# A second channel fold in the Fourier mixing of an attention and feed-forward kernel, with pooled rows packed into idle partitions and the local part added when the tokens are read back

## The chip, the cores and the metric

The kernel runs on one core of one Trainium2 chip. The metric is the device time of one execution in microseconds (us). A core has five engines with queues of their own, which run in order and wait for each other by semaphores: TensorE (PE; its weight loads are a row of their own, PEld), VectorE (DVE), ScalarE (ACT), GpSimd (POOL) and SyncE (SP), which here only issues DMAs. POOL issues some DMAs too, those that add to what lies at the destination.

## The reference

```python
# q, k, v: (8 batches, 8 heads, 576 positions, 64)
q_d, k_d, v_d = means of 4 neighbouring positions        # 144 groups
out_up    = repeat(softmax(q_d k_d^T / 8) v_d, 4)        # "pooled" attention
out_local = softmax(q k^T / 8 where |i - j| < 4) v       # "local" attention
x = (out_up + out_local) as (8, 576, 512)
u = x + real(fft(fft(x, axis=1), axis=2))                # sequence, then channels
un = (u - mean(u)) / sqrt(var(u) + 1e-6)                 # over the 512 channels
out = u + relu(un @ w1) @ w2                             # w1 512 x 2048, w2 2048 x 512
```

## The kernel before

For each batch the work has three parts: five units of local attention (`Unit`; a unit is two windows of 64 positions for all heads), four steps of pooled attention (`Pooled`; two heads each), and the mixing (`Mix`). The feed-forward (`Block`) follows, over nine blocks of 512 tokens and 16 slices `f` of the hidden layer. All fp32 products of the mixing and the feed-forward are made of three products of high and low parts (`fh` and `fl`, `yh` and `yl`, `hh` and `hl`).

No scheduler orders the instructions. Each class has a `plan` that puts its steps on a list with a number as its time (`at`), in units of a pace of 20 per batch; the list is sorted once, and each engine's queue is the sorted list cut down to that engine. The table `AT` holds the numbers. They set an order and nothing else.

The mixing, which the change is about, goes as follows. Local results lie in `xa` (positions of the first half) and `xb` (the second half, mirrored), as 3 slots of 128, 128 and 64 rows; the upper 64 rows of slot 2 hold zeros. `half_sum` (DVE) and `half_difference` (POOL) make `xs` and `xm`, the even and odd parts over the sequence. Pooled results lie in `odt`: 72 rows by 2, for the first and the mirrored second half. `channels_even` and `channels_odd` (DVE) fold the 512 channels into 256 sums and 256 differences (`xeo`); `split_high` (ACT) and `split_low` (POOL) make `fh` and `fl`. `sequence` then multiplies by cosines and sines over the sequence, in four groups `T` of 128 channels: 3 products of 5 slots (2 pooled slots of 72 rows, 3 local), 15 matmuls of 320 columns each, 60 in all; channel 256, which the fold leaves out, goes through `sequence_z` apart. `mix` multiplies by cosines and sines over the channels: for each of the 3 slots of output rows 7 matmuls of 512 columns for the even part and 6 for the odd, 39 in all. `mixed` (DVE) adds half of `xs` or `xm` to each, from PSUM (L611), `unfold` (POOL) makes sum and difference of the two (L621), and `store` (SP) writes these to `um` in DRAM, in 10 DMAs (L634, L635). The pooled results go to `ud` in DRAM, four copies of each row (L332, L336).

The feed-forward reads its tokens back: a load from `um` (SP, L706), and on top of it an adding load from `ud` (POOL, L704). The first block's tokens `ut` are loaded once the pooled part of the last batch is through (`close_b`, time `t_b`), and its norms begin at `t_a`, when the last local unit is through. The weights come as 64 `Quarter`s, each through a DMA (`raw`, L146), ACT, POOL, DVE (three instructions, L169 to L175), ACT and POOL; 12 of them are done during the attention, the others from `t_a` on.

A batch's queries and keys come by five DMAs (`qkT`, L361, on SP), and `sums` (DVE, L379) makes the pooled ones of them, for which the first product of a pooled step (`sp`, L262, on PE) waits.

Of the kernel before, what the change touches and what calls it, by code (L numbers as in the profile page):

```python
# [65 lines left out]
def kernel(  # L66
# [11 lines left out]
    c_group: bass.AP,  # L78
# [28 lines left out]
    um = [dram.tile([S + 1, DM], F32, name=f"um{b}") for b in range(B)]  # L107
# [21 lines left out]
    nc.vector.memset(mhalf, -0.5)  # L129
    ident = res.tile([P, P], F32, name="ident")  # L130
# [74 lines left out]
    odt = pd.tile([GH, 2, DM + 2], F32, name="odt")  # L205
# [34 lines left out]
    class Pooled:  # L240
# [74 lines left out]
        def result(self, h0):  # L315
# [7 lines left out]
                out=odt[:, :, h0 * D : (h0 + 2) * D].rearrange("g t (h d) -> g t h d", h=2),  # L323
# [4 lines left out]
        def store(self):  # L328

            for t in range(2):  # L330
                r0 = t * (HS + 1)
                nc.sync.dma_start(  # L332
                    out=ud[self.b][r0 : r0 + HS, :].rearrange("(g r) c -> g r c", r=4),
                    in_=odt[:, t, :DM].unsqueeze(1).to_broadcast([GH, 4, DM]),
                )
            nc.sync.dma_start(out=ud[self.b][HS : HS + 1, :], in_=odt[GH - 1 : GH, 1, :DM])  # L336

        def plan(self):
# [8 lines left out]
            at(pooled_end(b) + AT["store_pooled"][0], self.store)  # L347

# [143 lines left out]
    halves = [[pf.tile([P, NSL, DM + 2], F32, name=f"x{h}{i}") for h in "sm"] for i in range(2)]  # L492
    for t in (t for ts in halves for t in ts):
        nc.gpsimd.memset(t[:, :, DM:], 0.0)
    slots = [(t, P if t < NSL - 1 else W) for t in range(NSL)]

    def constants():
# [3 lines left out]
        nc.gpsimd.dma_start(out=seqg, in_=c_group)  # L501
# [4 lines left out]
    class Mix:  # L506


        def __init__(self, b):
            self.b, self.x, self.y = b, {}, {}  # L510
            self.fh = self.z = None


        def half_sum(self, t):
            self.xs, self.xm = halves[self.b % 2]
            nc.vector.tensor_add(out=self.xs[:, t, :DM], in0=xa[:, t], in1=xb[:, t])

# [5 lines left out]
        def source(self, t, odd):
            if t < NSL:
                return halves[self.b % 2][odd][:, t]
            return odt[:, t - NSL]

        def channels_even(self, t):
            x, src = psq.tile([P, DM], F32, name="xeo", bufs=2), self.source(t, 0)
            x = self.x[t] = x[: src.shape[0]]  # L530
            nc.vector.tensor_add(out=x[:, 0:HD], in0=src[:, 0:HD], in1=src[:, DM:HD:-1])
# [504 lines left out]
```

## Time and profile before

| | |
|---|---|
| median of 3 runs (lowest to highest) | 1250.11 us (1248.47 to 1251.0) |
| profiled execution: its time, its span | 1254.06 us, 1252.0 us |
| mean granted TensorE clock of that execution | 0.967 |
| busy PE, PEld | 1184.1 us (95%), 981.2 us (78%) |
| busy DVE, ACT, POOL | 590.7 us (47%), 356.0 us (28%), 318.2 us (25%) |
| DMA | 111.45 MB, mean 89 GB/s |

Every time below is from the profiled execution and counts from the start of its span. "Busy" is the time in which an engine had an instruction running; "idle before" is the gap ahead of an instruction and what ended it. A matmul's duration overlaps the next one's, so the price of a matmul in a row is the length of the row divided by their number. In the lines shown, names stand as written<-read; a row of a group ends with its busy time, the mean of one in ns, and the idle time before it with who ended it. The five last matmul groups of local values (`av`, L452) of a batch mark the end of its attention: they end at 56.7, 105.3, 157.7, 208.8, 258.8, 303.5, 348.7 and 389.0 us.

### The profile page before, as it was taken

Reading aid. Unit: us, or ns where it says so; the run is one execution under the profiler, and the core shown is the slowest. Engines: PE = TensorE matmul, PEld = TensorE weight load, DVE = VectorE, ACT = ScalarE, POOL = GpSimd, SP = SyncE. Lnnn points to the kernel's source line nnn. Section 1 sums busy time; section 2 is a strip of 40 time slices with the busy share of each in tenths; the row PEclk is TensorE's granted clock in tenths of the full one; section 3 lists DMA queues with packets and bytes.
Section 4 is the critical chain, followed back from the end, with each engine's and each line's share of the span. In section 5 each row is a group of like instructions: output and inputs, shape, how many; then the busy total and the mean of one; then the engine's idle time right before and its main releaser. Section 6 shows DMA issues by size and latency. Waiting matters only on the chain.

```text
span 1252.0 us, 20525 instructions
## 1 busy us (share of the span) xinstructions
PE 1184.1 (95%) x8336; PEld 981.2 (78%) x8336; DVE 590.7 (47%) x1218; ACT 356.0 (28%) x1038; POOL 318.2 (25%) x397
## 2 busy tenths in 40 slices
PE   5889998899995699999999999999999999999998
PEld 5777887787984578888888888888888888888887
DVE  3767778698877788853222222122122222221211
ACT  3655454555562333431111111111011111111100
POOL 2226355365456566531010010000100100100000
PEclk7888998999997799999999999999999999999999
DMA  9755484565645525314040120210400400300000
GB/s 293 197 169 134 128 238 110 162 196 172 163 127 153 133 77 155 119 51 101 5 97 1 52 50 1 78 25 1 99 3 1 101 1 1 101 1 1 34 1 34
DMA packets 50462, 111.45 MB, mean 89 GB/s; under 512 B 6120, under 2 KB 6248, under 8 KB 50040
## 3 DMA queue, kind: packets, MB, share of 16 engines
q1 hardware_dynamic: 42000, 88.66, 22.6%
q0 software_dynamic: 8368, 21.48, 9.3%
q8 instruction: 66, 1.08, 0.4%
q14 instruction: 28, 0.23, 0.1%
HBM read 81.82 MB, written 28.34 MB: 88 GB/s over the span
## 4 chain that ended last, share of the span: by engine, by line
PE 81%; DVE 10%; DMA 6%; POOL 1%; SPq 1%; issue 1%; ACT 1%; POOLq 0%
PE hps L761 31%; PE acc L779 10%; PE acc L781 10%; PE acc L780 10%; PE y L569 4%; PE mix L607 4%; DMA vsum<-in_vg_dram 3%; PE av L452 2%; DMA qkT<-in_qk_dram 2%; PE avd L307 2%; PE sc L393 1%; DVE sums L379 1%; DVE xeo L535 1%; PE tpn L732 1%; PE sp L262 1%
## 5 line engine op out<-in xcount | busy, mean ns | idle before, releaser
L761 PE MATMUL hps<-unT,w1h 128*128 128x512 f32 x1152 | 311.5, 392 | 0.6 <-DVE yl L578 0.6
L769 DVE SCALAR_TENSOR_TENSOR hl<-hps,hh 128x512 fp32r<-128x512 f32 x144 | 99.3, 690 | 437.3 <-ACT hh L765 437.3
L761 PEld LDWEIGHTS hps<-unT,w1h 128*128 128x128 f32 x1152 | 215.2, 188 | 46.7 <-DVE yl L578 0.8
L765 ACT ACTIVATE hh<-hps 128x512 fp32r<-128x512 f32 x144 | 86.2, 598 | 512.1 <-PE hps L761 512.0
L779 PE MATMUL acc<-w2h,hh 128*128 128x512 f32 x576 | 226.5, 393 | 0.0
L781 PE MATMUL acc<-w2h,hl 128*128 128x512 f32 x576 | 225.1, 391 | 0.0
L780 PE MATMUL acc<-w2l,hh 128*128 128x512 f32 x576 | 225.0, 391 | 0.0
L761 PE MATMUL hps<-unT,w1l 128*128 128x512 f32 x576 | 155.2, 391 | 0.0
L761 PEld LDWEIGHTS hps<-unT,w1l 128*128 128x128 f32 x576 | 108.1, 188 | 23.8
L781 PEld LDWEIGHTS acc<-w2h,hl 128*128 128x128 f32 x576 | 108.2, 188 | 23.6
L779 PEld LDWEIGHTS acc<-w2h,hh 128*128 128x128 f32 x576 | 108.1, 188 | 22.9
L780 PEld LDWEIGHTS acc<-w2l,hh 128*128 128x128 f32 x576 | 108.2, 188 | 22.8
L717 POOL TENSOR_TENSOR rstd<-rstd,mhalf 128x1 f32<-128x1 f32 x36 | 20.3, 564 | 341.4 <-DVE rstd L716 341.4
L704 POOL DMA_DIRECT2D ut<-ud x40 | 35.5, 1111 | 208.0 <-DMA ut<-um 207.7
L607 PE MATMUL mix<-chanm,yh 128*128 128x512 f32 (+1 forms) x192 | 65.8, 425 | 5.6 <-DVE xs L611 3.7
L411 ACT ACTIVATE sb<-sc,mx 128x64 f32<-128x64 f32 x320 | 69.8, 329 | 1.3
L741 DVE TENSOR_TENSOR unT<-tpn,unT 128x512 fp32r<-128x512 f32 x36 | 24.8, 690 | 90.4 <-ACT unT L738 90.4
L547 POOL TENSOR_TENSOR fl<-xeo,fh 128x512 fp32r<-128x512 f32 (+1 forms) x40 | 56.0, 1404 | 30.5 <-ACT fh L542 30.2
L379 DVE TENSOR_REDUCE sums<-qkT 128x224 f32<-128x896 f32 (+4 forms) x48 | 44.5, 947 | 27.9 <-DMA qkT<-in_qk_dram 19.6
L520 POOL TENSOR_TENSOR xm<-xa,xb 128x512 f32<-128x512 f32 x24 | 34.2, 1427 | 87.9 <-DVE xb L470 79.9
L738 ACT CAST unT<-tpn 128x512 fp32r<-128x512 f32 x36 | 21.0, 586 | 113.5 <-PE tpn L732 113.5
L452 PE MATMUL av<-vaug,pT 64*64 64x65 f32 x1280 | 48.5, 227 | 1.7 <-DVE odt L322 1.5
(102 smaller groups left out, 1579.7 us busy)
## 6 DMA issues: line engine op xcount, KB each, us to landing
qkT<-in_qk_dram SPq DMA_DIRECT2D x40, 512.0 KB
raw<-in_wq_dram SPq DMA_DIRECT2D x64, 256.0 KB
vaug<-in_vw_dram SPq DMA_DIRECT2D x40, 260.0 KB
ud<-odt SPq DMA_DIRECT2D x16, 576.0 KB
out_dram<-ut SPq DMA_DIRECT2D x36, 256.0 KB
ut<-um SPq DMA_DIRECT2D x32, 256.0 KB
ut<-ud POOLq DMA_DIRECT2D x32, 256.0 KB, 5.6
vsum<-in_vg_dram POOLq DMA_DIRECT2D x24, 292.5 KB, 4.5
```

The costliest lines, as they stand in the source:

```text
L379: nc.vector.tensor_reduce(out=to, in_=x[:, :, a - g0 : e - g0], axis=AX.X, op=ALU.add)
L411: nc.scalar.activation(out=self.sb[:, a], in_=self.sc[:, a * W : (a + 1) * W], func=AF.Exp, scale=0.125, bias=self.mx[:, a : a + 1],)
L452: nc.tensor.matmul(av[r, a, :], pT[r, 4 * hh + a], va[r, 4 * hh + a, :], start=True, stop=True)
L547: nc.gpsimd.tensor_sub(out=l, in0=self.x[t], in1=h.bitcast(F32))
L569: nc.tensor.matmul(y, l, r, start=(i == 0), stop=(i == len(mms) - 1))
L607: nc.tensor.matmul(to, l, r, start=(i == 0), stop=(i == len(mms) - 1))
L761: nc.tensor.matmul(hps, a[:, c, :], unT[:, x, c, :], start=(i == 0), stop=(i == len(mms) - 1))
L765: nc.scalar.activation(out=hh, in_=self.hps[f], func=AF.Relu)
L769: nc.vector.scalar_tensor_tensor(out=hl, in0=self.hps[f], scalar=0.0, in1=self.hh[f].bitcast(F32), op0=ALU.max, op1=ALU.subtract)
L779: nc.tensor.matmul(acc, hh, w2h, start=start, stop=False)
L780: nc.tensor.matmul(acc, hh, w2l, start=False, stop=False)
L781: nc.tensor.matmul(acc, hl, w2h, start=False, stop=stop)
```

## The change

The mixing is folded over the channels a second time. `channels` makes 255 sums and 255 differences into `w`; `fold` adds `w` to its own mirror image (DVE) and subtracts it from it (POOL), which leaves four groups of 128 channels, each of which reaches only the even or only the odd output channels. Two channels (0 and 256) now go through `sequence_z`. In `mix` each group has a product of 256 columns in place of 512: 1 matmul of 512 columns and 6 of 256 for the even part, 6 of 256 for the odd. `pack` moves the pooled results of the mirrored half by two SBUF to SBUF transfers: 56 rows into the idle rows 72 to 127 of `odt`, 16 rows into the idle rows 64 to 79 of `xa`'s slot 2. With that the pooled part is one slot, and a `sequence` group has 12 matmuls in place of 15.

`mixed` is gone. `even_out` (ACT) copies the even part from PSUM, and `unfold` (DVE) makes sum and difference of that copy and the odd part in PSUM, interleaving the two halves of 256 channels on the way. The local results are no longer added there: `store` writes `xa` and `xb` to a third DRAM tensor `ux` (10 more DMAs per batch on SP), and every block is loaded in three parts: `um` (SP), then adding loads from `ux` and from `ud` (POOL). `xs` and `xm` have one buffer each in place of two; the matrices of the channels shrink from 2 MB to 1 MB.

The first block's tokens have memory of their own from the start, and their loads are spread over the times 120 to 167; its norms begin at `t_b`, and the memory for its transposed tokens is there at `t_b` too.

```diff
-    "mix": (18.44, 18, 18),
+    "mix": (25.73, 25.9, 24.42, 25.37, 25.13),
-    "qk": (-11.61, 2.5),
+    "qk": (-10, 1.23),
...
+        def pack(self):
+            n = P - GH
+            nc.sync.dma_start(out=odt[GH:, 0, :DM], in_=odt[:n, 1, :DM])
+            nc.sync.dma_start(out=xa[W : W + GH - n, NSL - 1, :], in_=odt[n:GH, 1, :DM])
...
+        def channels(self, t, odd):
+            if self.w.get(t) is None:
+                self.w[t] = psq.tile([P, 2, HD], F32, name="w", bufs=2)
+            src = odt[:, 0] if t == NSL else halves[odd][:, t]
+            nc.vector.tensor_tensor(
+                out=self.w[t][:, odd, 1:HD], in0=src[:, 1:HD], in1=src[:, DM - 1 : HD : -1],
+                op=ALU.subtract if odd else ALU.add)
+        def fold(self, t, minus):
+            if self.x.get(t) is None:
+                self.x[t] = psq.tile([P, 4, P], F32, name="xeo", bufs=2)
+            eng, op = (nc.gpsimd, ALU.subtract) if minus else (nc.vector, ALU.add)
+            w = self.w[t]
+            eng.tensor_tensor(out=self.x[t][:, 2 * minus : 2 * minus + 2, :],
+                in0=w[:, :, 1 : P + 1], in1=w[:, :, HD - 1 : P - 1 : -1], op=op)
...
         def slots(self, x, odd, i):
-            groups = [(x[:GH, NSL + t], seqg[:, i, odd, t, :]) for t in range(2)]
-            return groups + [(x[:, t], seqm[:, i, odd, t, :]) for t in reversed(range(NSL))]
+            return [(x[:, t], seqm[:, i, odd, t, :]) for t in (NSL, NSL - 1, *range(NSL - 1))]
...
         def mix(self, t, odd):
-            for T in (2 * odd, 2 * odd + 1):
-                mms += [(lh, mh), (lh, ml), (ll, mh)]
-            if not odd:
-                mms.append((yz[:, cols], signs.unsqueeze(1).to_broadcast([P, HD, 2])))
+            if not odd:
+                sg = signs.unsqueeze(2).to_broadcast([P, 2, HD])
+                nc.tensor.matmul(to, yz[:, cols], sg, start=True, stop=False, skip_group_check=True)
+            for half, T in enumerate((3, 1) if odd else (0, 2)):
+                to = ps[:, half * HD : (half + 1) * HD]
+                for i, (l, r) in enumerate(((lh, mh), (lh, ml), (ll, mh))):
+                    nc.tensor.matmul(to, l, r, ...)
...
-        def mixed(self, t, odd):
-            x = (self.xm if odd else self.xs)[: slots[t][1], t, :DM]
-            nc.vector.scalar_tensor_tensor(out=x, in0=x, scalar=0.5, in1=self.ps, op0=ALU.mult, op1=ALU.add)
+        def even_out(self, t):
+            even = self.even[t] = pf.tile([P, DM], F32, name="even", bufs=2)
+            nc.scalar.copy(out=even[: slots[t][1]], in_=self.ps[t, 0])
-        def unfold(self, t):
-            for o, op in zip((oa, xm), (ALU.add, ALU.subtract)):
-                nc.gpsimd.tensor_tensor(out=o[:, t, :DM], in0=xs[:, t, :DM], in1=xm[:, t, :DM], op=op)
+        def unfold(self, t, minus):
+            even, ps = (x.rearrange("p (two n) -> p n two", two=2) for x in (self.even[t][:n], self.ps[t, 1]))
+            nc.vector.tensor_tensor(
+                out=self.o[minus][:n, t].rearrange("p (n two) -> p n two", two=2),
+                in0=even, in1=ps, op=ALU.subtract if minus else ALU.add)
...
+            at(..., self.store, ux, (xa, xb))
...
-                if pooled:
-                    nc.gpsimd.dma_start(out=u[r0 : r0 + m], in_=ud[b][k0 : k0 + m, :], accum_op=ALU.add)
+                src = (um, ux, ud)[part][b][k0 : k0 + m, :]
+                if part:
+                    nc.gpsimd.dma_start(out=u[r0 : r0 + m], in_=src, accum_op=ALU.add)
                 else:
-                    nc.sync.dma_start(out=u[r0 : r0 + m], in_=um[b][k0 : k0 + m, :])
+                    nc.sync.dma_start(out=u[r0 : r0 + m], in_=src)
...
-            at(t_b + 0.1 + 0.1 * i + AT["add"][0] * pooled, blocks[0].load, i, pooled)
+            at(120 + AT["add"][0] * part + 4 * i, blocks[0].load, i, part)
...
-            (blocks[0], t_a, AT["first_norms"]),
+            (blocks[0], t_b, AT["first_norms"]),
```

The table gives the queues another order at three places that matter below. The first is SP's queue in the middle of the program, around the five loads of the sixth batch's queries and keys. In the kernel before, where one of the loads has gone ahead of these rows and two follow:

```order
L361 DMA qkT<-in_qk_dram 128x1024
L634 DMA um_67<-oa 56x3x512
L634 DMA um_67<-oa 3x1x512
L634 DMA um_67<-oa 56x2x512
L634 DMA um_67<-oa 2x1x512
L635 DMA um_67<-oa 4x512
L634 DMA um_67<-xm_134 56x3x512
L634 DMA um_67<-xm_134 3x1x512
L634 DMA um_67<-xm_134 56x2x512
L634 DMA um_67<-xm_134 2x1x512
L635 DMA um_67<-xm_134 3x512
L361 DMA qkT<-in_qk_dram 128x1024
```

And in the changed kernel, the same place (line numbers are its own; `xb` is the local result, `o` the mixed one), where one load and the five stores of `xa` have gone ahead:

```order
L654 DMA ux_68<-xb 56x3x512
L654 DMA ux_68<-xb 3x1x512
L654 DMA ux_68<-xb 56x2x512
L654 DMA ux_68<-xb 2x1x512
L655 DMA ux_68<-xb 3x512
L375 DMA vaug<-in_vw_dram 128x520
L149 DMA raw<-in_wq_dram 128x512
L371 DMA qkT<-in_qk_dram 128x1024 x3
L375 DMA vaug<-in_vw_dram 128x520
L371 DMA qkT<-in_qk_dram 128x1024
L654 DMA um_75<-o_2982 56x3x512
```

Before, three of the five loads stand behind the store of the mixed rows; now four stand behind the store of the local results, and the mixed rows follow all five.

The second is VectorE's queue from the last pooled result of a batch to the folds. Before:

```order
L322 TENSOR_TENSOR odt<-avd,rsd 72x2x128
L406 TENSOR_REDUCE mx<-sc 128x8
L531 TENSOR_TENSOR xeo<-odt 72x256
L611 SCALAR_TENSOR_TENSOR xs_133<-xs_133,mix 128x512
L535 TENSOR_TENSOR xeo<-odt 72x256
L516 TENSOR_TENSOR xs_135<-xa,xb 128x512
L531 TENSOR_TENSOR xeo<-odt 72x256
L535 TENSOR_TENSOR xeo<-odt 72x256
```

And in the changed kernel, where `w` is what `channels` writes and `xeo` what `fold` writes:

```order
L325 TENSOR_TENSOR odt<-avd,rsd 72x2x128
L416 TENSOR_REDUCE mx<-sc 128x8
L476 TENSOR_SCALAR rs<-av 128x4 x2
L477 RECIPROCAL rs<-rs 128x8
L480 TENSOR_TENSOR xb<-av,rs 128x256 x2
L535 TENSOR_TENSOR w<-odt 128x255
L593 TENSOR_TENSOR yl<-y,yh 128x320
L535 TENSOR_TENSOR w<-odt 128x255
L548 TENSOR_TENSOR xeo<-w 128x256
L270 TENSOR_REDUCE mxd<-sp 72x2 x2
L636 TENSOR_TENSOR o_4493<-even,mix 128x512
L636 TENSOR_TENSOR o_4495<-even,mix 128x512
```

The folds of `odt`, which now wait for the transfer of `pack`, have moved five instructions away from the result; `o` is the new `unfold`, which has taken the place of `xs`, `xm` with `mix`.

The third is TensorE's queue at the end of the attention, behind the last local values and the last product of the seventh batch's mixing, where the eighth batch's `sequence` (`y`) and the first slice of the feed-forward (`hps`) follow. Before, with two more groups of `y` and four of `tpn` ahead of these rows:

```order
L569 MATMUL y<-seqg,fh 128x320 x2
L569 MATMUL y<-seqm,fh 128x320 x3
L569 MATMUL y<-seqg,fh 128x320 x2
L569 MATMUL y<-seqm,fh 128x320 x3
L569 MATMUL y<-seqg,fl 128x320 x2
L569 MATMUL y<-seqm,fl 128x320 x3
L761 MATMUL hps<-unT_5871,w1h_76 128x512 x4
L761 MATMUL hps<-unT_5871,w1l_77 128x512 x4
L761 MATMUL hps<-unT_5871,w1h_76 128x512 x4
```

And in the changed kernel:

```order
L753 MATMUL tpn<-ident,un 128x128 x4
L600 MATMUL yz<-seqm,z 4x320 x8
L753 MATMUL tpn<-ident,un 128x128 x8
L584 MATMUL y<-seqm,fh 128x320 x8
L584 MATMUL y<-seqm,fl 128x320 x4
L753 MATMUL tpn<-ident,un 128x128 x4
L782 MATMUL hps<-unT_5826,w1h_84 128x512 x4
L782 MATMUL hps<-unT_5826,w1l_85 128x512 x4
L782 MATMUL hps<-unT_5826,w1h_84 128x512 x4
L584 MATMUL y<-seqm,fh 128x320 x8
L584 MATMUL y<-seqm,fl 128x320 x4
```

The first slice of the feed-forward now stands behind one group of `y` in place of three.

More of the change, by code (lines that the diff above doesn't have):

```diff
@@ L129 @@
     nc.vector.memset(mhalf, -0.5)
+    uts = {0: [res.tile([P, DM], F32, name=f"ut0{i}") for i in range(TILES)]}
+    unTs = {}
     ident = res.tile([P, P], F32, name="ident")
@@ L523, in source @@
[L523 to L531, printed above, removed]
-        def channels_odd(self, t):
-            src = self.source(t, 1)
-            nc.vector.tensor_sub(out=self.x[t][:, HD:DM], in0=src[:, 0:HD], in1=src[:, DM:HD:-1])
+            nc.gpsimd.tensor_sub(out=halves[1][:, t, :DM], in0=xa[:, t], in1=xb[:, t])
@@ L627, in store @@
+        def store(self, to, xs):
+            for o, r0, first in ((xs[0], 0, 0), (xs[1], HS, 1)):
                 for n2 in range(2):
@@ L665, in plan @@
                 at(u + low, self.sequence_low, T)
-            first, step, mixed, unfold, store = AT["mixed"]
+            first, step, even, plus, minus, store = AT["mixed"]
             for i in range(NSL):
-                for odd in range(2):
-                    u = t + first + step * (2 * i + odd)
-                    at(u, self.mix, i, odd)
-                    at(u + mixed, self.mixed, i, odd)
-                at(u + unfold, self.unfold, i)
-            at(u + store, self.store)
+                u = t + first + step * 2 * i
+                at(u, self.mix, i, 0)
+                at(u + even, self.even_out, i)
+                at(u + step, self.mix, i, 1)
+                at(u + step + plus, self.unfold, i, 0)
+                at(u + step + minus, self.unfold, i, 1)
+            at(u + step + store, self.store, um, self.o)
+            at(4 * (NPAIR * self.b + NPAIR - 1) + AT["local_steps"][-1] + AT["store_local"][0], self.store, ux, (xa, xb))
     NU = B * NPAIR
@@ L693, in __init__, with load @@
             self.hps, self.hh, self.hl = {}, {}, {}
-        def load(self, i, pooled):
+        def load(self, i, part):
             u, tt = uts[self.n % 2][i], self.n * TILES + i
@@ L876 @@
             for i in range(TILES):
-                for pooled in range(2):
-                    at(starts[n] + 6 + 0.5 * i + 3 * pooled, blocks[n + 1].load, i, pooled)
+                for part in range(3):
+                    at(starts[n] + 6 + 0.5 * i + 2.5 * part, blocks[n + 1].load, i, part)
                 v = starts[n] + 12 + i * (t - starts[n] - 18) / TILES
```

198 lines of the change are left out of this document (99 added, 99 removed).

## The prediction

> **What bounds the kernel now.** I cut the span where the attention of each batch ends and read the busy time of the engines in each stretch (columns: stretch, its length, busy PE, PEld, DVE, ACT, POOL, then granted clock, DMA share, GB/s).
>
> ```profile
> 0.00:56.70 56.70, 38.10 (x562) 33.71 (x564) 30.53 (x71) 23.93 (x88) 14.26 (x29) 0.76 0.84 251
> 258.80:303.50 44.70, 43.27 (x588) 36.76 (x588) 39.05 (x89) 26.52 (x97) 24.21 (x27) 1.00 0.65 182
> 303.50:348.70 45.20, 43.35 (x590) 36.88 (x588) 40.33 (x89) 26.67 (x96) 25.04 (x27) 1.00 0.63 179
> 348.70:389.00 40.30, 40.16 (x532) 34.39 (x531) 30.79 (x77) 23.41 (x81) 20.75 (x23) 1.00 0.30 92
> 389.00:430.70 41.70, 17.64 (x85) 13.60 (x86) 27.53 (x57) 9.26 (x22) 28.70 (x35) 0.67 0.76 190
> 430.70:1252.00 821.30, 816.52 (x3639) 670.16 (x3638) 270.74 (x497) 137.85 (x272) 114.20 (x164) 1.00 0.17 46
> 56.70:389.00 332.30, 311.88 (x4055) 263.69 (x4052) 261.93 (x595) 184.93 (x657) 161.06 (x171) 0.96 0.56 156
> ```
>
> There are four stages. Up to 56.7 us loads come in (DMA share 0.84). Then seven batches take 332.3 us, 47.5 each; TensorE is busy 43.3 us per batch at full clock (second and third row), VectorE 261.93/7 = 37.4. So TensorE bounds this stage and VectorE is close behind. From 389.0 to 430.7 TensorE is mostly idle: the passage to the feed-forward. Behind it TensorE is busy 99% at full clock, and there only fewer matmuls would help; the change takes away none of the feed-forward's.
>
> The waits of 56.7 to 389 us, and the loads behind one of them (chain of waits and SP's queue):
>
> ```profile
> PE mix L607 <- DVE xs L611: 3.7, 3, 1.9
> PE sp L262 <- DVE sums L379: 2.5, 2, 1.3
> DVE sums L379 <- DMA qkT<-in_qk_dram: 11.6, 8, 3.0
> 270.55 2.39 SPq L634 DMA_DIRECT2D um<-oa  x4
> 276.41 0.36 SPq L361 DMA_DIRECT2D qkT<-in_qk_dram  x1
> 277.35 7.38 DMA qkT<-in_qk_dram
> 284.75 1.09 DVE sums L379
> ```
>
> VectorE waits 11.6 us for keys and queries, since their loads stand behind the store of the mixed rows on SP (276.41 is the first issue behind it; the load that takes 7.38 us releases the sums at once). The passage:
>
> ```profile
> 391.69 0.40 PE L607 MATMUL mix<-chanm,yl 128*64 128x512 f32 x1
> 405.01 0.69 DVE L713 BATCH_NORM_STATS2 st<-ut 128x6 f32<-128x512 f32 x1 [6.99 <-DMA ut<-ud]
> 408.39 1.09 PE L732 MATMUL tpn<-ident,un 128*128 128x128 f32 x4 [16.31 <-DVE un L724]
> 422.44 0.43 ACT L156 ACTIVATE wt<-raw 128x256 f32<-128x256 f32 x1 [7.07 <-DMA raw<-in_wq_dram]
> 424.43 0.90 PE L569 MATMUL y<-seqg,fh 72*128 72x320 f32 x2 [5.40 <-DVE unT L741]
> 430.68 1.10 PE L761 MATMUL hps<-unT,w1h 128*128 128x512 f32 x4
> ```
>
> TensorE stands 16.3 us, because VectorE waits 7.0 us for the first tokens, and 5.4 us more, because ScalarE waits for weights with the transposed tokens queued behind.
>
> **The change part by part.** TensorE first; both rows come from the chain of waits.
>
> ```profile
> 336.40 3.02 PE mix L607 x13
> 370.28 2.20 PE y L569 x15
> ```
>
> 512 columns cost 3.02/13 = 0.232 us, 320 cost 2.20/15 = 0.147. No row has 256. On the line through the two it is 0.119; in proportion to 512 it is 0.116 (one end), and no dearer than 320 (0.147, the other end). I take 0.119, as both ends lie near. Mixing per batch: 39 x 0.232 = 9.05 goes, 3 x 0.232 + 36 x 0.119 = 4.98 comes, so 4.07 less (4.2 to 3.1). Sequence: 60 to 48 matmuls saves 1.76, `sequence_z` 10 to 8 saves 0.29. Together 6.1 us per batch (5.1 to 6.2): 43.3 becomes 37.2.
>
> [...]
>
> VectorE, POOL and ScalarE per batch, from the groups:
>
> ```profile
> L611 DVE SCALAR_TENSOR_TENSOR xm<-xm,mix x24: 669/675/689, 96.8 to 466.1; 128x512 f32<-128x512 f32 x16, 64x512 f32<-64x512 f32 x8
> L531 DVE TENSOR_TENSOR xeo<-odt 72x256 f32<-72x256 f32 x16 | 14.7, 918 | 3.5 <-POOL fl L547 3.2
> L535 DVE TENSOR_TENSOR xeo<-odt 72x256 f32<-72x256 f32 x16 | 12.0, 749 | 0.0
> L531 DVE TENSOR_TENSOR xeo<-xs 128x256 f32<-128x256 f32 x24 | 13.0, 541 | 1.2 <-POOL fl L547 1.2
> L535 DVE TENSOR_TENSOR xeo<-xm 128x256 f32<-128x256 f32 x24 | 17.1, 714 | 0.0
> 58.15 0.68 DVE L406 TENSOR_REDUCE mx<-sc 128x8 f32<-128x512 f32 x1
> 57.81 0.41 DVE L531 TENSOR_TENSOR xeo<-odt 72x256 f32<-72x256 f32 x1
> L621 POOL TENSOR_TENSOR oa<-xs,xm 128x512 f32<-128x512 f32 x24 | 32.8, 1365 | 1.0 <-DVE xm L611 1.0
> L547 POOL TENSOR_TENSOR fl<-xeo,fh 72x512 fp32r<-72x512 f32 x16 | 24.6, 1543 | 7.9 <-ACT fh L542 7.7
> L547 POOL TENSOR_TENSOR fl<-xeo,fh 128x512 fp32r<-128x512 f32 x24 | 31.5, 1312 | 22.7 <-ACT fh L542 22.5
> L190 POOL TENSOR_TENSOR w1l<-wt,w1h 128x256 fp32r<-128x256 f32 x32 | 25.9, 810 | 24.5 <-ACT w1h L186 24.5
> L443 ACT COPY pT<-tpl 128x512 f32<-128x512 f32 x16 | 9.3, 584 | 9.8 <-PE tpl L423 9.8
> ```
>
> VectorE loses 6 `mixed` x 0.675 = 4.05 and 10 folds, 3 x (0.541 + 0.714) + 2 x (0.918 + 0.749) = 7.10. It gets 8 folds of 255, 8 x 0.63 (the mean of the two local forms) = 5.02, 4 second folds of 256 at 0.63 = 2.51 (0.41 alone to 0.92), and 6 `unfold`, which like `mixed` read one operand from PSUM: 6 x 0.675 = 4.05. Net +0.4. POOL loses 6 x 1.36 = 8.2 and 2 x 1.54 + 3 x 1.31 - 4 x 1.31 = 1.8 of low parts, and gets 4 differences of 256 at 0.81 = 3.2: net -6.8 of 23 us. That matters for VectorE, whose operations on SBUF alone stretch beside POOL's: a fold of `odt` takes 0.41 at 57.81, 0.918 on the mean. Over the folds and half sums this stretch is some 4 us per batch; with 30% less of POOL I take 1.2 off (0 to 2). ScalarE gets 3 copies of 0.584 and loses one split of some 0.62: +1.1 on 26.6, hidden.
>
> The new wait of VectorE is for `pack`. In the queue, five instructions lie between the result and the first fold of `odt`, some 2 us by their rows (the maxima alone 0.68). A transfer from SBUF to SBUF is in no row. The nearest are these (the last number is us from issue to landing):
>
> ```profile
> ut<-ud POOLq DMA_DIRECT2D x32, 256.0 KB, 5.6
> vsum<-in_vg_dram POOLq DMA_DIRECT2D x24, 292.5 KB, 4.5
> ```
>
> At best it lands within the 2 us, at worst after 5.6, a wait of 3.6. Its 144 KB are half of the second row's: I take 3 us, a wait of 1. Behind it stand the unfolds, and the maxima for which ScalarE waits. The second transfer, into `xa`, has the whole stretch up to `half_sum` as cover.
>
> So VectorE: 37.4 + 0.4 - 1.2 + 1.0 = 37.6 us per batch, TensorE 37.2. Two engines that wait for each other don't both reach 100%; the best busy share of VectorE in a stretch is 40.33/45.2 = 89%, with TensorE ahead of it. I take 91%, as fewer waits for keys and queries are left: 37.6/0.91 = 41.3 per batch, 7 x (47.5 - 41.3) = 43 us less. The ends are 38 per batch (TensorE alone, 67 less) and 46 (11 less).
>
> SP: 12 more DMAs per batch, 12 x 0.5 us of issuing (10 of the store of mixed rows go out from 270.55 to 276.4), with SP waiting most of the time: no cost by itself. The store of `xb` waits for a batch's last local result, with four loads of keys and queries and the next values behind it; between that result and the first sums VectorE has some 16 us of work in the queue, against 5 + 7.4 us for issuing and landing. The writing of `xa` by the next batch waits for the store of `xa`, which has about 10 us of VectorE's work as cover. DMA: 1.2 MB more per batch on 8 MB at a share of 0.6, hidden.
>
> The passage: the tokens' loads are over long before, so the 7.0 us go, and the raw weights are asked for earlier. What is late next is the last mixing: behind the last local values VectorE has one result, six folds, three second folds, three half sums, four unfolds, four statistics and a norm, some 15 us, then ScalarE and POOL. So `y` begins some 16 us after 389 and the first slice some 18.5, where it was 41.7, with two groups of `y` (3.6 us) still to come: 19.6 less. Against that, POOL's adding loads double (5 more ahead of the weights' steps, each waiting for the one below, 4.5 to 5.6 us), and VectorE waits for POOL behind that. I set one such landing, 5.6 us, against the 19.6 and take 14 less (8 with two, 19.6 with none). Further on, the last batch's rest of `sequence` and mixing saves 0.45 + 4.07 = 4.5. In the feed-forward the third load comes at most 5.6 us later per block, ahead of a block's first statistics by about nothing, and a late one delays no matmul unless by over 3 us: 0.
>
> Sum: 43 + 14 + 4.5 = 62 less than 1254.06, the profiled execution's time, so 1192; the median of the runs, 1250.11, lies 4 lower, and 1188 is the prediction.
>
> **The rivals.** (1) TensorE alone is the bound, at 38 us a batch, and the passage gives 18: 67 + 18 + 4.5 = 89 less, 1161. For it: 40.16 of 40.3 us busy in the last stretch. Against it: VectorE has less to do there (30.79).
>
> (2) `pack` lands late: 3.6 us of wait in place of 1, so 40.2/0.91 = 44.2 per batch, 23 + 14 + 4.5 = 42 less, 1209.
>
> (3) `unfold` reads one channel from each half in turn, 1 KB apart in SBUF, and pays double: 6 x 0.675 = 4.05 us more, 45.8 per batch, 12 + 14 + 4.5 = 30 less, 1220. No row has such a reading; one operand comes from PSUM, as in L611. [...]
>
> (4) Slower: the loads of keys and queries come late behind the store of `xb`. If TensorE stood for all of it (5.3 us of issues and 7.4 of landing, each batch), a batch would take 37.2 + 12.7 = 49.9, and some 2 us of half clock on top 52: 32 more, less 18.5 from the end, 1264. It decides from 50.1 us per batch on. Against it stand the 16 us of cover.
>
> (5) The gain of TensorE's is there but VectorE and the passage eat it: within noise.
>
> **How the numbers follow.** The forecast's case (1172 to 1204) has 0.56, (1) 0.14, (2) 0.13, (3) 0.10, (4) 0.05, (5) 0.02. The range, 1164 to 1218, holds the forecast, (2) and half of (1) and (3), and leaves out 0.19. A change within 0.2% (2.5 us) couldn't be told from none. Faster is 0.93, same 0.02, slower 0.05.
>
> **What would show it.** A matmul of 256 columns at 0.12 us; 37 us of TensorE and 37 to 39 of VectorE per batch, 40 to 42.5 us apart; `unfold` at 0.68; a wait of about 1 us of the first fold for `pack`; no 3 us waits of the sums; the first `hps` some 18 us behind the last local values; the feed-forward as dense as now. I am wrong if VectorE's waits for transfers or its stretched operations put a batch above 44 us, or if TensorE's busy share reaches 97% again.

## The result and the profile after

The changed kernel takes 1198.88 us (median of 4 runs, 1195.12 to 1200.32) where the one before takes 1250.55 (4 runs, 1248.47 to 1253.69): a ratio of 0.958, 95% interval 0.955 to 0.961. The prediction was 1188, in a range of 1164 to 1218. The profiled execution took 1200.32 us, with a span of 1198.5.

Its stages, cut as before where the last local values of a batch end (57.8, 101.3, 143.6, 188.1, 231.8, 275.4, 314.5 and 349.9 us) and at the first slice (376.7); the columns are those of the prediction's first fence:

```profile
0.00:57.80 57.80, 39.67 (x611) 35.05 (x612) 27.93 (x65) 25.98 (x97) 9.85 (x23) 0.79 0.74 225
57.80:101.30 43.50, 36.82 (x548) 32.26 (x549) 38.60 (x90) 27.37 (x98) 20.69 (x26) 0.92 0.70 206
231.80:275.40 43.60, 38.36 (x574) 34.61 (x574) 38.98 (x90) 28.42 (x102) 19.46 (x25) 0.96 0.80 228
275.40:314.50 39.10, 37.26 (x573) 33.42 (x573) 34.65 (x84) 25.06 (x88) 17.33 (x22) 1.00 0.91 264
314.50:349.90 35.40, 32.42 (x484) 29.76 (x482) 28.57 (x73) 23.43 (x83) 17.07 (x21) 1.00 0.65 158
57.80:349.90 292.10, 262.12 (x3894) 233.80 (x3894) 262.63 (x613) 187.99 (x659) 135.73 (x164) 0.96 0.77 219
349.90:376.70 26.80, 10.96 (x64) 9.26 (x63) 25.17 (x45) 6.96 (x16) 18.31 (x22) 0.68 0.72 205
376.70:1198.50 821.80, 815.63 (x3659) 671.37 (x3659) 274.91 (x514) 142.78 (x284) 143.78 (x204) 1.00 0.25 58
```

The seven batches went from 332.3 to 292.1 us, the passage from 41.7 to 26.8; the start is 1.1 longer, and what follows the first slice 0.5 longer. The batches are 41.7 us apart on the mean, but not evenly: the first five 42.3 to 44.5, the sixth 39.1, the seventh 35.4. TensorE is busy 262.12/7 = 37.4 us per batch, VectorE 262.63/7 = 37.5, and now neither is near the 96 to 97% that TensorE had in two of the prediction's rows: each is busy 90%.

The prices within the batches: the chain of waits first, then VectorE's groups (busy us, mean of one in ns, idle before), VectorE's waits (us, times, longest), and the durations of three lines (shortest/median/longest in ns):

```profile
332.99 1.76 PE y L584 x12
...
347.36 1.48 PE mix L623 x12
```

```profile
L636 DVE TENSOR_TENSOR o<-even,mix 128x512 f32<-128x512 f32 x25 | 16.4, 691 | 0.8 <-PE mix L623 0.7
L548 DVE TENSOR_TENSOR xeo<-w 128x256 f32<-128x256 f32 x29 | 18.6, 640 | 1.4
L535 DVE TENSOR_TENSOR w<-xs 128x255 f32<-128x255 f32 x21 | 17.9, 853 | 0.2
L524 DVE TENSOR_TENSOR xs<-xa,xb 128x512 f32<-128x512 f32 x21 | 18.8, 894 | 0.0
L389 DVE TENSOR_REDUCE sums<-qkT 128x224 f32<-128x896 f32 x12 | 12.9, 1076 | 0.0
```

```profile
DVE w L535 <- DMA odt<-odt: 9.4, 8, 2.8
DVE yl L593 <- ACT yh L590: 6.6, 6, 2.1
DVE mxd L270 <- PE sp L265: 2.3, 4, 0.9
```

```profile
L636 DVE TENSOR_TENSOR o<-even,mix x37: 673/687/712, 99.3 to 349.4; 128x512 f32<-128x512 f32 x25, 64x512 f32<-64x512 f32 x12
L535 DVE TENSOR_TENSOR w<-xs x21: 404/756/1381, 62.6 to 328.3; 128x255 f32<-128x255 f32 x21
L524 DVE TENSOR_TENSOR xs<-xa,xb x21: 674/684/1654, 61.2 to 324.7; 128x512 f32<-128x512 f32 x21
```

A matmul of 256 columns costs 1.48/12 = 0.123 us. `unfold` (L636), strided reading and all, takes 0.69. The sums (L389) wait for no load of keys any more (0.0). The folds wait 9.4 us in 8 times, 1.2 each, for `pack`.

The passage, from the timeline of the three engines:

```profile
358.01 1.02 POOL L548 TENSOR_TENSOR xeo<-w 128x256 f32<-128x256 f32 x1
358.11 2.70 DVE L524 TENSOR_TENSOR xs<-xa,xb 128x512 f32<-128x512 f32 x1
358.70 1.55 POOL L527 TENSOR_TENSOR xm<-xa,xb 128x512 f32<-128x512 f32 x1
...
368.52 1.08 PE L753 MATMUL tpn<-ident,un 128*128 128x128 f32 x4 [15.17 <-DVE un L745]
...
369.14 0.98 DVE L548 TENSOR_TENSOR xeo<-w 128x256 f32<-128x256 f32 x1
...
373.09 1.90 PE L584 MATMUL y<-seqm,fh 128*128 128x320 f32 x8
...
376.69 1.20 PE L782 MATMUL hps<-unT,w1h 128*128 128x512 f32 x4 [0.68 <-ACT unT L759]
```

VectorE's waits for tokens are gone. It is busy 25.17 of 26.8 us, and TensorE stands 15.2 us for its first norm.

### The profile page after: what moved, and what is told of

Read it like the earlier page. It is cut to its first block, busy times and chain, and to the rows that moved or that the text cites. A ratio compares the mean times of both kernels' runs of the same rounds, so it can differ in the third digit from the quotient of the medians.

```text
span 1198.5 us, 20501 instructions
## 1 busy us (share of the span) xinstructions
PE 1128.4 (94%) x8224; PEld 949.5 (79%) x8224; DVE 590.6 (49%) x1234; ACT 363.7 (30%) x1054; POOL 307.7 (26%) x410
## 4 chain that ended last, share of the span: by engine, by line
PE 74%; DVE 11%; DMA 6%; issue 4%; POOL 2%; ACT 1%; SPq 1%; DVEq 0%; POOLq 0%; ACTq 0%
PE hps L782 32%; PE acc L802 11%; PE acc L800 11%; PE acc L801 11%; PE y L584 3%; DMA vsum<-in_vg_dram 2%; DVE w L535 1%; DVE o L636 1%; PE tpn L753 1%; DMA ux<-xa 1%; DVE xs L524 1%; PE av L462 1%; DVE sums L389 1%; DMA raw<-in_wq_dram 1%; PE sc L403 1%
## 5 line engine op out<-in xcount | busy, mean ns | idle before, releaser
L725 POOL DMA_DIRECT2D ut<-ux x40 | 35.7, 1106 | 205.7 <-DMA ut<-um 205.5
L403 PEld LDWEIGHTS sc<-qkT 64*64 64x64 f32 x1280 | 48.0, 146 | 3.8 <-issue 1.2
L562 POOL TENSOR_TENSOR fl<-xeo,fh 128x512 fp32r<-128x512 f32 x32 | 44.8, 1401 | 13.7 <-ACT fh L559 13.7
L403 PE MATMUL sc<-qkT 64*64 64x64 f32 x1280 | 48.0, 230 | 0.0
L389 DVE TENSOR_REDUCE sums<-qkT 128x224 f32<-128x896 f32 (+4 forms) x48 | 43.2, 943 | 8.6 <-DMA qkT<-in_qk_dram 8.6
L462 PEld LDWEIGHTS av<-vaug,pT 64*64 64x64 f32 x1280 | 42.9, 140 | 5.4 <-DMA vaug<-in_vw_dram 4.5
```

Of the source, the lines that this page charges most:

```text
L389: nc.vector.tensor_reduce(out=to, in_=x[:, :, a - g0 : e - g0], axis=AX.X, op=ALU.add)
L403: nc.tensor.matmul(sc[r, a * W : (a + 1) * W], self.qkT[r, 0, a // 2, o : o + W], self.qkT[r, 1, a // 2, o : o + W], start=False, stop=Tru ...
L462: nc.tensor.matmul(av[r, a, :], pT[r, 4 * hh + a], va[r, 4 * hh + a, :], start=True, stop=True)
L562: nc.gpsimd.tensor_sub(out=self.fl[:, t], in0=self.x[t], in1=self.fh[:, t].bitcast(F32))
```

## The experiments

All were timed against the kernel before. The start is left out of the comparison by stage: in the profiled executions it took between 52.7 and 58.7 us, whatever the kernel. "First five" is the mean distance of the first five of the seven batches. The columns by stage come from one profiled execution of each kernel.

| kernel | median, us | ratio to before, 95% | first five | 6th, 7th | seven batches | passage | rest |
|---|---|---|---|---|---|---|---|
| before | 1250.55 | 1 | 49.4 | 45.2, 40.3 | 332.3 | 41.7 | 821.3 |
| changed | 1198.88 | 0.958 (0.955 to 0.961) | 43.5 | 39.1, 35.4 | 292.1 | 26.8 | 821.8 |
| no_pack | 1192.15 | 0.954 (0.949 to 0.958) | 43.4 | 38.9, 37.7 | 293.6 | 26.2 | 821.2 |
| one_unfold | 1196.56 | 0.957 (0.952 to 0.961) | 43.8 | 40.4, 35.1 | 294.6 | 24.3 | 821.4 |
| mix_512 | 1209.43 | 0.967 (0.962 to 0.971) | 44.4 | 43.1, 37.6 | 302.7 | 26.0 | 824.1 |
| no_ux | 1194.23 | 0.954 (0.950 to 0.958) | 43.4 | 38.9, 35.4 | 291.1 | 26.6 | 820.7 |
| raw_once | 1199.50 | 0.957 (0.955 to 0.959) | 43.9 | 39.5, 36.5 | 295.3 | 26.8 | 821.8 |
| no_decode | 1191.84 | 0.951 (0.949 to 0.953) | 40.9 | 42.2, 35.2 | 281.7 | 26.8 | 821.2 |
| late_block0 | 1214.47 | 0.968 (0.965 to 0.972) | 43.5 | 38.8, 35.2 | 291.5 | 42.3 | 821.0 |
| early_norms | 1197.76 | 0.955 (0.952 to 0.958) | 43.5 | 39.7, 38.8 | 296.1 | 16.5 | 823.1 |
| mix_less | 1196.02 | 0.956 (0.953 to 0.960) | 42.9 | 42.6, 36.0 | 293.2 | 26.9 | 820.1 |
| both_less | 1194.11 | 0.954 (0.952 to 0.957) | 42.0 | 40.3, 36.1 | 286.5 | 25.3 | 820.6 |
| best1 | 1194.94 | 0.955 (0.953 to 0.957) | 43.8 | 43.1, 35.6 | 297.7 | 8.6 | 832.8 |
| best3 | 1193.60 | 0.953 (0.951 to 0.956) | 43.7 | 43.8, 33.7 | 296.0 | 8.6 | 833.8 |

Theory V is the prediction's: VectorE's work, at 91% busy, sets the distance of the batches. The first four runs put it and its rivals to the test.

**no_pack**

```diff
-            at(pooled_end(b) + 0.05, self.pack)
```

> Leaves out pack: the 72 pooled rows of the mirrored half are not moved (zeros stand in their place), all else is as in the changed kernel, whose stages are 57.8 us (start), 292.1 (seven batches), 26.8 (passage), 821.8 (feed-forward). Theory V (VectorE's queue sets the pitch of the batches): the 9.4 us in which the folds of odt wait for the transfer come back almost whole, the seven batches take 282 to 284 us, the whole 8 to 10 us less than the changed kernel. Rival T (TensorE sets the pitch, VectorE's wait only uses up slack): the batches stay within 2 us of 292, the whole within 3.

The batches took 293.6 us, not 282 to 284: V is refuted on this point, and T's figure for the batches (within 2 us of 292) holds. The wait that the prediction had priced rightly was not on the path. VectorE waits elsewhere instead (lines of no_pack, to be compared with 6.6 and 2.3 in the changed kernel):

```profile
DVE yl L592 <- ACT yh L589: 10.0, 9, 2.1
DVE mxd L270 <- PE sp L265: 7.3, 7, 1.9
```

The run's median is 6.7 us under the changed kernel's, but the intervals overlap, and behind the start the three stages sum to 1141.0 against 1140.7.

**one_unfold**

```diff
-                at(u + step + minus, self.unfold, i, 1)
```

> Leaves out the second unfold (the difference; the sum is stored to both halves): VectorE has 3 x 0.69 = 2.1 us less per batch, 35.4 in place of 37.5, TensorE's 37.4 and all else stay. Theory V: the pitch falls from 41.7 to between 39.4 (VectorE at 90% busy) and 40 (TensorE next), the seven batches take 276 to 281 us, and the passage, in which VectorE is busy for 25.2 of 26.8 us, loses some 1.4 (the two unfolds that stand in it); the whole 12 to 18 us less. Rival T: the batches stay within 3 us of 292, the whole within 5.

The row of the batches (the same columns):

```profile
54.20:348.80 294.60, 265.12 (x3894) 237.04 (x3894) 254.20 (x595) 188.01 (x659) 135.16 (x164) 0.95 0.76 217
```

VectorE has 8.4 us less to do in this stretch, and it is no shorter, as T expected: VectorE alone doesn't set the distance. In the passage it does: 24.3 in place of 26.8.

**mix_512**

```diff
-                to = ps[:, half * HD : (half + 1) * HD]
+                to = ps.rearrange("p (two n) -> p two n", two=2)
...
-                        to, l, r, ...
+                        to, l, r.unsqueeze(1).to_broadcast([P, 2, HD]), ...
```

> Each product of the mixing runs over 512 columns again (the 256 read twice, the result is not used as such): TensorE has 36 x 0.113 = 4.1 us more per batch, 41.5 in place of 37.4; VectorE's 37.5 and all else stay. Theory V: TensorE takes over as the bound at 95 to 97% busy, a pitch of 43 to 43.7 in place of 41.7, 9 to 14 us more in the seven batches and 4 behind them: 13 to 18 us more than the changed kernel. Rival T (TensorE sets the pitch now): all of it shows, 28.5 + 4 = 33 us more. Second rival (VectorE alone counts): 0 to 4 in the batches, 4 behind them.

```profile
52.70:355.40 302.70, 283.47 (x3894) 240.34 (x3895) 259.74 (x614) 188.08 (x659) 134.48 (x164) 0.97 0.75 213
```

10.6 us more in the batches and 2.3 in the rest; the median is 10.6 longer, where V had 13 to 18 and T 33. So T is refuted here, and for the batches the number is V's, but the place isn't: the first five rise by 0.9 us each, and the sixth and seventh, where TensorE was busy 95% and 92%, by 4.0 and 2.2. Of 28.5 us that the shorter products save over seven batches, 10.6 show at this point. Against the kernel before, the batches are still 29.6 us shorter (332.3 to 302.7): most of the gain is there without the shorter products. What the other parts give, above all the 14 fewer matmuls per batch over the sequence and the new order of the queues, no run takes apart.

**no_ux**

```diff
-            at(4 * (NPAIR * self.b + NPAIR - 1) + ... , self.store, ux, (xa, xb))
...
+            if part == 1:
+                return
```

> Leaves out the third DRAM tensor: local results are neither stored nor added when tokens are read (10 DMAs less per batch on SP, 4 to 5 adding loads less per block on POOL). Theory V: the transfers are hidden, the batches keep their 292 us but for some 4 us in which TensorE waits for values loaded behind that store in the second batch; the passage is bound by VectorE's work and stays at 26 to 27; the whole 0 to 5 us less. Rival D (the DMA engines, 70 to 91% busy in the batches, hold loads back, and POOL's adding loads hold the passage back by a landing of 5.6): 10 or more less in the batches and 5 in the passage, 15 or more in the whole.

The batches, the passage and the rest are shorter by 1.0, 0.2 and 1.1 us, within V's bound; rival D is refuted. The third tensor costs a few us at most, and the landing that the prediction set into the passage is not there.

The next question was why the first five batches stand 43.5 us apart when no one engine's work shows. They differ from the sixth by the 12 weight quarters that are decoded meanwhile.

**raw_once**

```diff
-                nc.sync.dma_start(out=self.raw..., in_=src...)
+                if self.n == 0 or self.f >= CHUNKS[0]:
+                    nc.sync.dma_start(out=self.raw..., in_=src...)
```

> Of the 12 weight quarters that are decoded during the attention only the first is loaded; the other eleven are decoded again from the same data, with all their work on ScalarE, POOL, VectorE (so the weights of the first three slices are not the right ones). Before it, less work for VectorE (2 us per batch) and no wait for pack had each left the first five pitches at 43 to 44 us, while the sixth batch, where nothing is decoded, takes 39. Theory R (a raw load stands in SP's queue behind stores and pack, ScalarE waits for it, and TensorE behind ScalarE): the first five pitches fall to 39 to 41.5, the whole 10 to 20 us less than the changed kernel's 1199. Rival W (the decode's work sets the pitch, not its loads): within 4 us. Rival Q (the decode has no part in it): within 4 us here, and the next run the same.

The first five stay at 43.9. Theory R is refuted: the loads of raw weights, which stand in the chain of waits (4.82 and 5.93 us at 216 and 230), set nothing.

**no_decode**

```diff
-            decode(n, first + step * n, ahead)
+            for part in wts[x.f, x.w]:
+                if x.j == 0:
+                    nc.gpsimd.memset(part..., 0.0)
```

> Leaves out the 12 early quarters altogether (zeros stand for the weights of the first three slices): no raw loads until the attention's end, and some 20 us less of VectorE's work with its stretch, 10 of ScalarE's, 16 of POOL's over the batches. Theory R and rival W both: the first five pitches fall from 43.5 to 38 to 40, the seven batches take 268 to 278 in place of 292, the whole 14 to 24 less; R expects as much from the run without the loads alone, W expects it here only. Rival Q (loads of keys, queries and values, or the chain of steps from scores to results, set the pitch): within 5 us of 292.

```profile
58.60:340.30 281.70, 260.87 (x3894) 233.71 (x3894) 245.89 (x577) 179.45 (x635) 118.08 (x140) 0.96 0.76 216
```

281.7: 10.4 us less, where R and W expected 14 to 24 and Q at most 5. The first five come to 40.9, and the sixth takes 42.2 (TensorE stands 1.8 us there for values loaded late). With 16.7 us less for VectorE, 17.7 for POOL and 8.5 for ScalarE the batches gain 10.4, so the decoding's work (W) has a part in the distance, but not as one engine's sum.

**late_block0**

```diff
-            at(120 + AT["add"][0] * part + 4 * i, blocks[0].load, i, part)
+            at(t_b + 0.1 + 0.1 * i + 0.5 * part, blocks[0].load, i, part)
```

> Undoes one part: the first block's three loads per tile go out at the time of its norms again, not during the attention. Theory P (VectorE's work in its queue, 25 of 26.8 us, sets the passage, and the early loads keep the statistics from waiting): the first tile is whole three loads later, some 2.5 + 5.7 + 5.3 us behind the issue, VectorE stands 4 to 10 us for it with the last mixing behind, the passage takes 31 to 37 in place of 26.8, the whole 4 to 10 more than the changed kernel. Rival (the loads would be hidden anyway): passage and whole within 2.

VectorE's longest wait and the row of the passage:

```profile
DVE st L734 <- DMA ut<-ud: 16.7, 1, 16.7
```

```profile
350.20:392.50 42.30, 10.37 (x64) 8.45 (x62) 24.02 (x44) 6.88 (x16) 24.42 (x28) 0.64 0.78 197
```

15.5 us more in the passage, which is then as long as before the change (41.7): with three loads per tile and the statistics where the changed kernel has them, the early loads are worth the whole of the passage's gain, and more than the expected 4 to 10, because VectorE waited 16.7 us for the first tile's third part.

**early_norms**

```diff
-    "first_norms": (1.77, 1.54, 6.94, 0.87),
+    "first_norms": (-8, 1.0, 0.3, 0.6),
-    "ffn": (5.97, 1.6),
+    "ffn": (3.0, 1.6),
-            at(120 + AT["add"][0] * part + 4 * i, blocks[0].load, i, part)
+            at(100 + AT["add"][0] * part + 4 * i, blocks[0].load, i, part)
-ROUND = 5
+ROUND = 6
```

> The first block's loads 20 units of the table earlier, its statistics ahead of the last local units, its norms right behind the pooled part, the slices of the feed-forward 3 units earlier, six in the first round in place of five: the same work, with the first block's norms on VectorE ahead of the last mixing in place of behind it. Theory P: the first slice no longer waits for the last mixing; it begins some 12 to 16 us behind the last local values in place of 26.8, and TensorE does hps of two slices (6 us) in what was idle time; the mixing itself ends no later by more than 3; the whole 3 to 8 us less than the changed kernel. Rival (the feed-forward then waits for decoded weights or for the last mixing all the same): the first slice early, the whole within 2.

The first slice came 16.5 us behind the last local values, and the last pitch (the distance of the last two batches) grew by 3.4, as the turning of the first tile now stood ahead of the last local values on TensorE and waited for its norm. Over the three stages 5.0 us less; in the median 1.1, inside the intervals and within the 2 of the rival.

**mix_less** and **both_less** asked whether the two engines are tied, so that less work for one shows nothing and less for both does. mix_less has the edit below, both_less this one and that of one_unfold.

```diff
-                for i, (l, r) in enumerate(((lh, mh), (lh, ml), (ll, mh))):
+                for i, (l, r) in enumerate(((lh, mh),)):
```

> Leaves out two of the three products of the mixing over the channels (24 matmuls of 256 columns per batch): TensorE has 24 x 0.119 = 2.9 us less per batch, 34.6 in place of 37.4; VectorE's work stays. Known before it: 2.1 us less of VectorE's work per batch left the batches at 294.6 (292.1 with it), 4.1 us more of TensorE's gave 302.7. Theory C (the two are tied: in the first five batches VectorE is busy for 40 and TensorE for 38.5 of 43.6 us, each waits for the other in a fixed order, and work taken from one alone shows by less than half): the seven batches take 283 to 290. Rival T (TensorE sets the pitch after all): 272 to 276. Rival L (a chain of latencies, no engine's work): 290 to 294. Behind the batches 3 us less in any case.

```profile
55.00:348.20 293.20, 252.85 (x3742) 222.53 (x3742) 259.99 (x612) 186.79 (x658) 133.29 (x162) 0.92 0.77 218
```

293.2: T is refuted, and C by its number too; L's 290 to 294 holds. The stretch has 152 matmuls fewer (3894 to 3742), some 18 us at the 0.119 of the expectation; TensorE's busy time fell by 9.3, with the granted clock at 0.92 in place of 0.96, and the batches took as long as before. The first five gain 0.6 each, and the sixth loses 3.5, with a pause of 1.7 us for late values and a mean clock of 0.91 from 275 to 315 us, where the changed kernel has no wait above 1.3 us and a clock of 1.00.

> Leaves out both: the second unfold (2.1 us per batch of VectorE) and two of the three products of the mixing (2.9 of TensorE). Theory C: together they show far more than the two alone (which would be +2.5 and 2 to 9 less), the seven batches take 270 to 280. Rival T: as with the products alone, 272 to 276 in both. Rival L: 287 to 294, as little as each alone.

286.5, 5.6 us less than the changed kernel: more than the two alone (294.6 and 293.2), but far from the 270 to 280 of C and just under the 287 of L. A tie of the two explains a small part at most. What the runs support, without showing it, is L in a weak form: the order of steps across the engines holds the first five batches near 43 us.

**best1** and **best3** follow the traces' waits to a better order. The first diff is against early_norms, the second against best1.

```diff
-    "first_norms": (-8, 1.0, 0.3, 0.6),
+    "first_norms": (-8, 1.0, 0.5, 0.6),
...
-                at(t + d, fn)
+                at(t + d + 4 * (self.b == B - 1), fn)
```

> early_norms, mended at the two places where its trace showed new waits: its first norm 0.2 units later, so that the turning of the first tile stands behind the last local values on TensorE and not ahead of them (there TensorE stood 2.3 us, and the last pitch was 38.8 in place of 35.4), and the last batch's product of channels 0 and 256 4 units later, so that the first slice doesn't stand behind it (7.8 us of wait). Theory P (VectorE's order sets the passage, TensorE has slack in it): the last pitch 35.5 to 36.5, the first slice 12 to 14 us behind the last local values, the whole 8 to 12 us less than the changed kernel. Rival (the last mixing, 20 us of VectorE's work, still ends where it did, and the slices only move about): within 4.

The last pitch is 35.6 and the first slice comes after 8.6 us, earlier than expected; but the rest grew by 11.0 us, as the last mixing now lies there and TensorE stands in it 4.8 us for ScalarE's split of a late fold and 2.4 for transposed tokens. Passage and rest together lose 7.2 us, and the sixth batch gives back 4.0 (with a pause of 2.4 us for values). In the median it is 3.9 us under the changed kernel, where P expected 8 to 12: the rival's case.

```diff
+                    late = len(these) > 1 and i == 1 and self.b < B - 1
-                    at(u + high, self.split_high, slot)
-                    at(u + low, self.split_low, slot)
+                    at(u + high + 1.05 * late, self.split_high, slot)
+                    at(u + low + 0.6 * late, self.split_low, slot)
-    "load_v": (4.22,),
+    "load_v": (3.6,),
```

The ground for it, in the changed kernel's trace (timeline of ScalarE and TensorE, then busy time in slices of 4 us):

```profile
200.49 0.62 ACT L559 CAST fh<-xeo 128x512 fp32r<-128x512 f32 x1 [3.79 <-POOL xeo L548]
...
201.68 1.50 PE L291 MATMUL tp<-ident,sd 72*72 72x72 f32 x8 [4.56 <-ACT sd L281]
```

```profile
194.00:198.00 4.00, 3.11 (x72) 2.90 (x68) 3.95 (x5) 1.90 (x5) 3.94 (x4) 1.00 0.77 274
198.00:202.00 4.00, 0.33 (x2) 0.19 (x3) 3.94 (x10) 1.48 (x5) 2.45 (x2) 0.76 0.86 254
202.00:206.00 4.00, 4.00 (x26) 2.18 (x27) 3.79 (x5) 3.12 (x14) 3.41 (x5) 0.50 0.89 328
```

TensorE stands 4.56 us, and its clock is 0.50 for the first 5 us behind that.

> best1 with two moves in the table, both at pauses of TensorE that come back in every run so far. In the third and fourth pitch of the changed kernel (and of all variants) TensorE stands 2 to 5.5 us for the pooled exponentials (sd), because ScalarE, in order, waits up to 3.8 us ahead of them to split a fold that POOL makes only when VectorE's folds w are through; for batches one to seven that split (the middle slot) now goes behind the exponentials. And the values (vaug) are loaded 0.62 units earlier, ahead of the store of the local results on SP, for whose sake TensorE stands 2.4 and 1.6 us in the first pitch. Theory H (such pauses, not the sum of any engine's work, make the first five pitches 43 to 44 us, and each also costs a slot of half clock behind it): those pauses go or fall under 1.5 us, the first five pitches come to 40 to 42.5 on the mean (best1: 43.8, the changed kernel 43.5), the seven batches to 280 to 292 (best1: 297.7), the whole 6 to 14 us less than best1. Rival (the pause moves to the next place, where the delayed split is waited for): the first five stay at 43 to 44.5, the whole within 4 of best1.

TensorE's waits from 53 to 350 us in best3:

```profile
PE tp L291 <- ACT sd L281: 4.4, 3, 2.2
PE av L462 <- DMA vaug<-in_vw_dram: 4.2, 2, 2.9
PE mix L623 <- ACT sd L281: 2.6, 1, 2.6
```

The pause of 4.56 us fell to 2.2, the others stayed, and the first five stayed at 43.7: the rival, not theory H. 1193.60 and 1194.94 are the lowest medians among the kernels that leave nothing out, but the changed kernel's interval (0.955 to 0.961) touches theirs: no better version is shown.

**What stays open.** Which ring of steps holds the first five batches at 43 to 44 us. The wait for `pack`, the store of the local results, the raw loads, 2 us of VectorE's work and 3 of TensorE's each moved them by under 1 us, both engines' work together by 1.5, and all of the decoding by 2.6. The chain of waits gives no single answer either. In the changed kernel it spends 4.7% of its time on the store of the local results (`ux`) and 3.7% on raw loads, 14 and 11 us if taken over the batches; without the one the batches are 1.0 us shorter, without the other 3.2 longer. When one link goes, others make a chain of nearly the same length.

## Why the prediction was right, and where it was wrong

| term | forecast | measured | from |
|---|---|---|---|
| start | 0 | +1.1 | 56.7 to 57.8 |
| seven batches | -43 | -40.2 | 332.3 to 292.1 |
| passage, less two groups of `y` moved behind it | -14 | -11.3 | 41.7 - 26.8 - 3.6 |
| rest of the last batch and the feed-forward | -4.5 | -3.1 | 821.8 - 821.3 - 3.6 |
| sum | -61.5 | -53.5 | span 1252.0 to 1198.5 |

The profiled execution of before lay 4 us above its median, that of the changed kernel 1.4: with that and with rounding the 8 us grow to the 10.9 between 1188 and 1198.88.

**The prices held.** 0.123 us for 256 columns (0.119 taken), 37.3 us of TensorE in the sixth batch, at full clock like the rows that the forecast started from (37.2; the mean of all seven is 37.4), and 37.5 of VectorE per batch (37.6), `unfold` at 0.69 (0.675), a wait of 1.2 us for `pack` (1; six instructions lie ahead of that fold, not five, but they take the 2 us that were counted), no wait of the sums for keys. VectorE's stretch fell too: over the folds, half sums and decoding, their time above the shortest of their form, from 36 to 31 us in seven batches, 0.7 per batch (1.2 taken).

**The batches: the size held by luck, the reason didn't hold.** The step was "37.6/0.91 = 41.3 per batch"; it came out at 41.7, with VectorE 90% busy. But of the seven distances only one (42.3) lies in the 40 to 42.5 that were named, and taking 2.1 us of VectorE's work or the whole wait for `pack` away made the batches no shorter. 41.7 is the mean of five batches at 43.5, which no engine's work sets alone, and two at 39.1 and 35.4, where TensorE is busy 95% and 92%. That looks like rival (1)'s case, but it is only half borne out: with more work for TensorE (mix_512) the two grew by 4.0 and 2.2, with less (mix_less) they didn't shrink (42.6 and 36.0). A busy share was read as a bound that it isn't. Rivals (2) and (3) fell: the folds waited 1.2 us for the transfer, not 3.6, and that wasn't on the path; no run shows the doubled price of (3), an assumption, and the strided reading shows no cost (0.69 against 0.675). (4) fell with the sums' wait at 0.0; its 2 us of half clock were an estimate: in the trace of before the clock was 0.50 for 3.8 us behind the stand of 5.40 that ended at 424.43.

**The passage: both sizes were wrong, in opposite ways.** The step "some 15 us, then ScalarE and POOL" for VectorE's list was too short. From 349.9 the last fold ended at 369.14 + 0.98, 20.2 us later, and `y` began at 373.1 and the slice at 376.7, 23.2 and 26.8 us behind, not 16 and 18.5. VectorE's groups in the passage show where:

```profile
L524 DVE TENSOR_TENSOR xs<-xa,xb 128x512 f32<-128x512 f32 x3 | 5.1, 1711 | 0.0
L745 DVE TENSOR_SCALAR un<-ut,mv,rstd 128x512 f32<-128x512 f32 x4 | 4.3, 1084 | 1.0 <-issue 1.0
```

Three half sums took 5.1 us where three of the shortest take 2.0: the one at 358.11 took 2.70 beside the two POOL instructions in the timeline. The six folds `w` took 4.0 where six of the shortest (0.40) take 2.4, and the norm at 366.76 took 1.61 where the shortest takes 0.53. The list was priced without the stretch that was counted in the batches. On the other side, the 5.6 us for a landing of POOL's adding loads didn't occur: without the loads of `ux` the passage takes 26.6. The errors partly cancel, 11.3 against 14: the passage's total came out nearer than either of its terms. That the 7.0 us of VectorE's wait would go was right, and too little: three-part loads at the time of the norms cost 16.7.

**The rest.** TensorE's work there fell as forecast (816.52 to 815.63 busy, with 3.6 us of `y` moved in), but its idle time rose from 4.8 to 6.2 us.

## What to carry to other kernels

Before dividing an engine's work by a busy share, ask whether the share is a bound: here two engines at 90% in a fixed order of steps gave back nothing when either got less to do (294.6 and 293.2 us against 292.1), and a run with work left out shows it. A load for the next stage is worth moving early when the first instruction that needs it stands in an in-order queue ahead of work on the critical path: here that was 15.5 us, the whole gain of the stage. And where an engine's list is priced beside a busy neighbour, take the durations from such a place, not the shortest ones: here a half sum took 2.70 us beside POOL and 0.67 at the shortest.

## What the runs showed of the hardware

VectorE's instructions with both operands in SBUF stretched beside POOL's. Of the 64 folds `w` (L535) of the execution, the 35 that ran while POOL had nothing running took 0.41 to 0.43 us; the other 29 took 0.89 in the median and up to 1.50. L524 took 0.67 to 2.70. `unfold`, with one operand in PSUM, took 0.67 to 0.71 in all 48 cases, 38 of them beside an instruction of POOL. The norm (L745), with a single large input in SBUF, stretched in some cases all the same:

```profile
L745 DVE TENSOR_SCALAR un<-ut,mv,rstd x36: 531/546/1656, 366.8 to 1082.4; 128x512 f32<-128x512 f32 x36
```

The two that took 1.61 and 1.66 us ran beside POOL's `fl`. Why these stretched isn't shown.

Less work for TensorE didn't make it earlier where it then waits: in mix_less its busy time fell by 9.3 us, the granted clock from 0.96 to 0.92, and the batches took as long; with more work (mix_512) the clock was 0.97. One execution says little of this, as kernels with all the matmuls had 0.93 (best1) to 0.96 in the batches. But over four executions each the clock of the whole was 0.962 to 0.971 in mix_less, 0.969 to 0.979 in the changed kernel and 0.975 to 0.985 in mix_512. Behind the pause of 4.56 us, which ended at 201.68, the clock was 0.50 up to 206, and 1.00 from 207 on. It was also 0.50 from 108 to 111, where the longest single gap ahead was 1.03 us: TensorE had been busy 2.41 of the 4 us before (104 to 108). So here short gaps came ahead of half the clock too.

A transfer of 112 KB from SBUF to SBUF, which no row of before had, stands in the chain of waits with 2.5 us at 94.8 and 5.0 at 305.6:

```profile
94.81 2.52 DMA odt<-odt
...
305.63 4.98 DMA odt<-odt
```
